# Moving scores, values and a projection's halves in the TensorE order of three turns

## The chip, the cores and the metric

The kernel runs on one core of a Trainium2 chip. The metric is the device time of one execution in microseconds, as the median of three runs. The core has five engines that work from queues of their own, each strictly in the order in which its instructions stand: TensorE (PE in the profile, with its weight loads as PEld), VectorE (DVE), ScalarE (ACT), GpSimd (POOL) and SyncE (SP, which here only issues DMAs). They wait for each other by semaphores.

## The reference, cut to what matters

Two blocks follow each other. The first is a gated linear attention with a state of 48 by 48 per head: 4 batches, 8 heads, 768 steps.

```
for t in range(S):
    state = alpha[:, :, t, :, None] * state + einsum('bhd,bhe->bhde', k[:, :, t], v[:, :, t])
    y[:, :, t] = einsum('bhd,bhde->bhe', q[:, :, t], state)
```

Its output, heads side by side, is x with 384 columns. The second block projects x to 512 values and 512 gates, runs a first-order recurrence over the values, multiplies with the SiLU of the gates and projects back:

```
proj = x @ w_in;  val, gate = proj[..., :512], proj[..., 512:]
h = a * h + val[:, t, :];  ys[:, t, :] = h          # for every t
out = (gate * sigmoid(gate) * ys) @ w_out
```

All arrays are float32 at this level (the weights come as 64-bit floats and are converted on the chip).

## The kernel before

The steps are cut into 12 groups of 256 steps, three to a batch. One pass of the loop at L1051, called a **turn** here (n = 0 is the first), projects group n and at the same time does the attention of group m = n + 1, so that the two can fill each other's waits. `general` (L19 to L332) is a second version for unusual inputs, chosen by a flag at the end; it doesn't run here.

The attention of a group has these parts, named by the helpers:

- **Preparation on VectorE**, `products` (L656): alpha is transposed (`turn`, L594), P is a running product over it (`scan_P`, L625), k is transposed, V is a running sum from the other end (`scan_V`, L642), Zk is k times V, q is transposed, Zq is q times P. For groups 4 and up these are seven steps of a generator; `go(count)` (L978) issues the next ones, so its place in the code is their place in VectorE's queue. They are the steps for group n + 2. For groups 1 to 3 the transposes are done on TensorE (`turned`, L684), in one of two forms: as transposes (L689, L690), or as matmuls with the identity (L694).
- **Scores**, `first(m)` (L1031): `scores` (L733) are 32 matmuls of 48 by 64 by 112 into two fixed banks and two rotating ones. `masks` (L748) follows: VectorE masks one half (A, L759), ScalarE copies the other (AK, L760) and GpSimd masks it (L762), ScalarE copies the parts for the states (K, L764).
- **Values and states**, `second(m)` (L1036): `values` (L766) needs both masked halves; `states` (L795) makes the new parts of the state, which ScalarE copies (dS, L818) and GpSimd adds up (`add_up`, L820). In the first two groups VectorE adds them instead (`add_banks`, L832).
- **Carried**, `third(m)` (L1042): the products of q with the added-up states (`carried`, L782) and the rest of the values, then `join` (L900), which brings the result to xT over ScalarE and DMAs on SyncE and GpSimd.

The projection has four parts, `project(n, cc)` (L915). Each is three matmuls of 128 by 128 by 256 for the values into one bank and three for the gates into another; VectorE runs the recurrence over the values (hh, L932), ScalarE the SiLU of the gates (sg, L940), and the returned function multiplies the two (f, L942), on VectorE in the first two turns and the last, on GpSimd else. `output(n)` (L945) is 16 matmul passes of 384 columns and two copies.

A float32 matmul stands in the trace as two passes, each with a weight load; a transpose stands as one.

**What sets the order.** The whole fast version is under a manual schedule: the order of the Python calls is the order on every engine. The rotating banks are four (`ps_mm`), taken in pairs: two calls later the same pair comes again, and its new user waits until VectorE and ScalarE have read the old content. So projection 3 of a turn waits for hh and sg of projection 1 of that turn, and projection 2 for those of projection 0.

In turns 2 to 10 the order on TensorE is: second(m), project 0, 1, 2, 3, third(m), first(m + 1), output(n). In turn 2 first(3) stands at the turn's beginning (L1125), and projection 0 of that turn goes between scores and values. VectorE's steps of `go` come four ahead of projection 0 (one and two in turn 2), then one ahead of each further projection.

Of the kernel before, what the change touches and what calls it, by code (L numbers as in the profile page):

```python
# [346 lines left out]
def fast(  # L347
# [22 lines left out]
    nc = tc.nc  # L370
# [9 lines left out]
    NK = DM // C  # L380
# [300 lines left out]
    def bank_pair(tag=None):  # L681
        return [bank(tag and f"{tag}{i}") for i in range(2)]

    def turned(m, name, js, t):  # L684
        raw = steps_of(name, m)
        tp = t[:, 0:len(js) * C].rearrange("p (j x) -> p j x", j=len(js))
        if (m, name) in ((1, "k"), (1, "q"), (3, "a")):
            for n, j in enumerate(js):
                nc.tensor.transpose(tp[:, n], raw[:, ds(ROW + j * D - 64, C)], ident)  # L689
                nc.tensor.transpose(tp[0:64, n], raw[:, ds(j * D, 64)], ident)  # L690
            return tp.rearrange("p j (c h) -> p h c j", h=4)
        for n, j in enumerate(js):
            for i in range(2):
                nc.tensor.matmul(tp[ds(64 * i, 64), n], raw[:, ds(i * ROW + j * D, 64)], ident,  # L694
                                 start=True, stop=True, skip_group_check=True)
        return tp.rearrange("p j (c h) -> p h c j", h=4)
# [69 lines left out]
    def values(m, across):  # L766

        v_sb = vs[m % NV]
        if across:
            ys[m] = [t.rearrange("p (e t) -> p e t", e=2) for t in bank_pair("y")]  # L770
        for c in range(G):
            for e in range(2):
                for h in range(2):
                    i = 1 - h if across else h
                    for s in range(2):
                        p = 2 * e + (s ^ i)
                        rows = ds(L * h, L)
                        nc.tensor.matmul(ys[m][i][ds(64 * s, 64), e, ds(c * C + h * L, L)],  # L778
                                         v_sb[rows, c, 4 * i + p, :], As[i][rows, c, p, :],
                                         start=across and c == 0 and e == 0, stop=False, skip_group_check=True)  # L780
# [131 lines left out]
    prev_h = [None] * NI  # L912
    fs = {}

    def project(n, cc, late=False):  # L915
# [10 lines left out]
        for vg, kk in order:  # L926
            nc.tensor.matmul((pv, pg)[vg], w_ins[cc][:, kk, vg, :], xT[:, kk, :],  # L927
                             start=(kk == 0), stop=(kk == NK - 1))
        hh = p2.tile([C, GC], FP32, tag=f"h{cc}", name="hh")

        def scan():
            nc.vector.tensor_tensor_scan(  # L932
                out=hh, data0=a_dec[:, cc:cc + 1].to_broadcast([C, GC]), data1=pv,
                initial=prev_h[cc][:, GC - 1:GC] if n % NG else 0.0, op0=ALU.mult, op1=ALU.add)
            prev_h[cc] = hh

        if not late:
            scan()
        sg = p2.tile([C, GC], FP32, tag="sg", name="sg")
        nc.scalar.activation(sg, pg, AF.Silu)  # L940
        engine = nc.vector if n < 2 or n == N - 1 else nc.gpsimd
        f = lambda: engine.tensor_mul(fs[n][cc], sg, hh)  # L942
        return (scan, f) if late else f
# [34 lines left out]
    def go(count):  # L978
        for _ in range(count):
            next(steps, None)  # L980
# [15 lines left out]
    for js, part in zip(halves, parts):  # L996
        copy_turned(tk, js, part)
    low(0)
    parts = [turned(1, "q", js, bank()) for js in halves]
    convert(0)  # L1000
    nc.gpsimd.memset(raws["a"][0:1, 0:1], 0.0)
    load_steps("a", 2, [nc.sync])
# [4 lines left out]
    st = states(0)  # L1007
# [34 lines left out]
    def third(m):  # L1042
        if m < N:
# [4 lines left out]
            if m >= NG:  # L1048
                add_up(m, (3,))

    for n in range(N):  # L1051
        m = n + 1
        if n == 0:
# [17 lines left out]
            convert(3)  # L1071
            junk(1)
            low(4)
            f2 = project(n, 2)
            values(m, True)
            st = states(m)
            add_banks(m, st)
            alphas(3)
            third(m)
            for name in "qa":  # L1080
# [42 lines left out]
        else:  # L1123
            if n == 2:
                first(m)  # L1125
                go(1)
                f0 = project(n, 0)
                second(m)
                go(2)
            else:  # L1130
                second(m)
                go(4)
                f0 = project(n, 0)
            f0()
# [93 lines left out]
```

## Time and profile before

| what | us |
| --- | --- |
| median of 3 runs | 279.72 (278.26 to 280.07) |
| the profiled execution | 279.43 |
| its span, first to last instruction | 277.7 |
| TensorE busy | 268.8 |
| VectorE busy | 218.3 |
| GpSimd busy | 122.4 |
| ScalarE busy | 108.6 |

The profiled execution ran 1.7 us longer than its span, and its time is 0.3 us below the median. All times in rows count from the span's start. A row of the chain of waits has start, duration and what ran or was waited for; "issue" is time in which the trace shows nothing to wait for. A row of the timeline has start, duration, engine, line, operation, output and inputs with their shapes, and in brackets the idle time before it. Matmuls are pipelined, so the rows of the chain, which give each group's part of the elapsed time, are better for sums than the durations of single ones. The clock granted to TensorE was 1.0 throughout.

### The profile page before, as it was taken

How to read it: one execution, taken by the hardware profiler on the slowest of the kernel's cores; microseconds unless marked ns; L12 is line 12 of the kernel's file. 1: busy time of each engine (PE TensorE's matmuls, PEld its weight loads, DVE VectorE, ACT ScalarE, POOL GpSimd, SP SyncE). 2: the span in 40 equal slices, each digit the busy share in tenths (PEclk: the TensorE clock that was granted, in tenths of full speed). 3: DMA queues.
4: the chain of work that ended last, by engine and by line, in shares of the span. 5: the costliest groups of instructions: out<-in, count | busy, mean ns of one | idle time of the engine just before them, and what ended most of it. 6: DMA issues, size and time to landing. Idle time of an engine off the chain costs nothing.

```text
span 277.7 us, 9598 instructions
## 1 busy us (share of the span) xinstructions
PE 268.8 (97%) x4056; PEld 217.0 (78%) x4056; DVE 218.3 (79%) x281; ACT 108.6 (39%) x244; POOL 122.4 (44%) x141
## 2 busy tenths in 40 slices
PE   7999999999989999899999999999999999999995
PEld 5988887876678688488688688688688688787874
DVE  7979998898798995995895995996995993079540
ACT  2577763461332532341542433433434425213111
POOL 8141223130068574563473584484384476435000
PEclk9999999999999999999999999999999999999999
DMA  6949993845919777487468587576687501201201
GB/s 196 295 140 309 296 262 78 205 88 139 267 48 238 149 199 182 103 214 163 103 181 199 114 205 164 130 197 155 152 186 159 144 0 27 77 1 33 71 5 59
DMA packets 51599, 41.18 MB, mean 148 GB/s; under 512 B 27360, under 2 KB 49536, under 8 KB 51552
## 3 DMA queue, kind: packets, MB, share of 16 engines
q1 hardware_dynamic: 48752, 37.50, 53.1%
q0 software_dynamic: 1408, 2.03, 2.8%
q10 hardware_dynamic: 1392, 0.99, 1.2%
q8 instruction: 33, 0.54, 0.9%
q14 instruction: 14, 0.11, 0.2%
HBM read 32.54 MB, written 4.72 MB: 134 GB/s over the span
## 4 chain that ended last, share of the span: by engine, by line
PE 92%; DVE 3%; DMA 1%; POOL 1%; issue 1%; ACT 1%; SPq 0%; DVEq 0%; ACTq 0%
PE mm L927 45%; PE mm L956 21%; PE y L791 4%; PE y L778 4%; PE mm L744 3%; PE s L744 3%; PE s L810 3%; PE mm L694 2%; PE mm L1189 2%; DMA raw_a<-in_alpha_dram 1%; POOL AK L762 1%; DVE P L630 1%; DVE V L649 1%; PE mm L689 1%; PE y L862 1%
## 5 line engine op out<-in xcount | busy, mean ns | idle before, releaser
L927 PE MATMUL mm<-xT,w_in 128*128 128x256 f32 x576 | 128.9, 382 | 0.6 <-ACT xT L884 0.6
L927 PEld LDWEIGHTS mm<-xT,w_in 128*128 128x128 f32 x576 | 108.1, 190 | 16.3 <-issue 0.8
L956 PE MATMUL mm<-w_out,f_last 128*128 128x384 f32 x160 | 54.1, 492 | 1.3 <-DVE A L759 1.3
L940 ACT ACTIVATE sg<-mm 128x256 f32<-128x256 f32 x48 | 18.4, 384 | 85.8 <-PE mm L927 80.3
L956 PEld LDWEIGHTS mm<-w_out,f_last 128*128 128x128 f32 x160 | 29.7, 190 | 21.1 <-issue 1.4
L830 POOL TENSOR_TENSOR sum<-sum,dS 128x192 f32<-128x192 f32 x30 | 33.2, 1108 | 27.3 <-PE mm L927 13.5
L942 POOL TENSOR_TENSOR f_last<-sg,hh 128x256 f32<-128x256 f32 x36 | 30.9, 862 | 30.6 <-ACT sg L940 23.1
L932 DVE TENSOR_TENSOR_SCAN hh<-a_dec,hh,mm 128x256 f32<-128x256 f32 x32 | 23.4, 732 | 15.4 <-PE mm L927 15.2
L630 DVE TENSOR_TENSOR_SCAN P<-al,lower 128x1028 f32<-128x1028 f32 x12 | 31.1, 2595 | 0.6
L649 DVE TENSOR_TENSOR_SCAN V<-al,ends 128x1028 f32<-128x1028 f32 x12 | 28.3, 2356 | 0.4
L907 POOL DMA_DIRECT2D xT<-yst x40 | 20.5, 517 | 13.1 <-ACT yst L904 11.8
L950 ACT ACTIVATE o_sb<-mm 128x384 f32<-128x384 f32 x22 | 10.8, 491 | 38.4 <-PE mm L956 38.4
L762 POOL TENSOR_TENSOR AK<-AK,mask 128x512 f32<-128x512 f32 x9 | 13.2, 1464 | 17.2 <-ACT AK L760 17.2
L759 DVE TENSOR_TENSOR A<-s,mask 128x256 f32<-128x256 f32 x9 | 3.8, 425 | 21.5 <-PE s L744 21.5
L557 POOL TENSOR_TENSOR w_in<-w_in,wr 128x768 int32<-128x768 int32 x4 | 7.3, 1826 | 26.0 <-DVE wr L555 17.0
L595 DVE STREAM_TRANSPOSE k<-raw_k 128x1024 f32<-128x1024 f32 x9 | 18.3, 2033 | 0.0
L595 DVE STREAM_TRANSPOSE q<-raw_q 128x1024 f32<-128x1024 f32 x9 | 18.2, 2022 | 0.0
L778 PEld LDWEIGHTS y<-AK,v 64*64 64x64 f32 x352 | 12.1, 134 | 6.4 <-issue 5.0
L595 DVE STREAM_TRANSPOSE al<-raw_a 128x1024 f32<-128x1024 f32 x8 | 16.3, 2041 | 0.1
L778 PE MATMUL y<-AK,v 64*64 64x64 f32 x352 | 14.5, 221 | 1.0 <-POOL AK L762 1.0
L791 PEld LDWEIGHTS y<-Zq,sum 48*64 48x64 f32 x656 | 11.8, 134 | 4.3 <-issue 4.1
L791 PE MATMUL y<-Zq,sum 48*64 48x64 f32 x656 | 14.4, 221 | 0.6 <-issue 0.6
(158 smaller groups left out, 392.2 us busy)
## 6 DMA issues: line engine op xcount, KB each, us to landing
v<-in_v_dram SPq DMA_DIRECT2D x22, 192.0 KB, 3.3
out_dram<-o_sb SPq DMA_DIRECT2D x22, 192.0 KB, 2.1
raw_k<-in_k_dram SPq DMA_DIRECT2D x18, 184.0 KB, 3.4
raw_q<-in_q_dram SPq DMA_DIRECT2D x18, 184.0 KB, 3.8
raw_k<-in_k_dram SPq DMA_DIRECT2D x18, 176.0 KB, 3.8
raw_q<-in_q_dram SPq DMA_DIRECT2D x18, 176.0 KB, 4.1
raw_a<-in_alpha_dram SPq DMA_DIRECT2D x16, 184.0 KB, 5.0
raw_a<-in_alpha_dram SPq DMA_DIRECT2D x16, 176.0 KB, 5.1
```

The costliest lines, as they stand in the source:

```text
L595: nc.vector.transpose(out=by_runs(to).rearrange("p h c j -> p h j c"), in_=raws[name][:, 0:4 * ROW].rearrange("p (h j d) -> p h j d", h=4, ...
L630: nc.vector.tensor_tensor_scan(out=P, data0=al[:, 0:4 * GP], data1=lower.rearrange("p h t -> p (h t)"), initial=0.0, op0=ALU.mult, op1=ALU ...
L649: nc.vector.tensor_tensor_scan(out=V[:, ::-1], data0=al[:, 1:4 * GP + 1][:, ::-1], data1=ends.rearrange("p h t -> p (h t)")[:, ::-1], init ...
L778: nc.tensor.matmul(ys[m][i][ds(64 * s, 64), e, ds(c * C + h * L, L)], v_sb[rows, c, 4 * i + p, :], As[i][rows, c, p, :], start=across and ...
L791: nc.tensor.matmul(ys[m][i][ds(64 * s, 64), e, ds(u * L, L)], Ss[j][rows, p, :], Zqs[m % 2][rows, u, p, D:], start=False, stop=True, skip_ ...
L830: nc.gpsimd.tensor_add(Ss[j][:, :, 0:D], Ss[j - 1][:, :, 0:D], part)
L907: engines[n % len(engines)].dma_start(out=xT[to, a], in_=st[rows, i, e])
L927: nc.tensor.matmul((pv, pg)[vg], w_ins[cc][:, kk, vg, :], xT[:, kk, :], start=(kk == 0), stop=(kk == NK - 1))
L932: nc.vector.tensor_tensor_scan(out=hh, data0=a_dec[:, cc:cc + 1].to_broadcast([C, GC]), data1=pv, initial=prev_h[cc][:, GC - 1:GC] if n % ...
L940: nc.scalar.activation(sg, pg, AF.Silu)
L942: f = lambda: engine.tensor_mul(fs[n][cc], sg, hh)
L956: nc.tensor.matmul(os[c], fs[n][cc][:, ds(c * C, C)], w_outs[cc // 2][:, cc % 2, :], start=(cc == 0), stop=(cc == NI - 1))
```

## The change

Four things are moved; nothing is added to or taken from what is computed.

1. **Start**: the second half of q of group 1 is turned by eight matmuls with the identity instead of eight transposes.
2. **Turn 0**: projection 2 is parted. Its three value matmuls and the recurrence come first, then values and states of group 1 and the additions of the states, then its three gate matmuls and the SiLU.
3. **Turns 2 and 4** (the third and the fifth): values and states of groups 3 and 5 stand behind projection 1 instead of behind projection 0 (turn 2) or ahead of it (turn 4). In turn 4 two of the four `go` steps now stand behind projection 0. The functions f of projections 0 and 1 come ahead of `add_up` on GpSimd in both turns.
4. **Turn 3** (the fourth): the scores of group 5 and their masks stand behind output 3 instead of ahead of it.

```
-        if (m, name) in ((1, "k"), (1, "q"), (3, "a")):
+        if (m, name) in ((1, "k"), (1, "q"), (3, "a")) if by_transpose is None else by_transpose:
...
-    parts = [turned(1, "q", js, bank()) for js in halves]
+    parts = [turned(1, "q", js, bank(), js is halves[0]) for js in halves]
...
+        passes(order[:NK] if between else order)
...
         if not late:
             scan()
+        if between:
+            between()
+            passes(order[NK:])
         sg = p2.tile([C, GC], FP32, tag="sg", name="sg")
...
+    late = (1, 3)
...
-            f2 = project(n, 2)
-            values(m, True)
-            st = states(m)
-            add_banks(m, st)
+            def across_and_states():
+                values(m, True)
+                add_banks(m, states(m))
+
+            f2 = project(n, 2, between=across_and_states)
...
             if n == 2:
                 first(m)
-                go(1)
-                f0 = project(n, 0)
-                second(m)
-                go(2)
-            else:
+            if n - 1 not in late:
                 second(m)
                 go(4)
-                f0 = project(n, 0)
+            else:
+                go(n // 2)
+            f0 = project(n, 0)
             f0()
+            if n - 1 in late:
+                go(2)
             load_raw("k", n + 3, nc.sync)
             load_raw("a", n + 3, nc.sync)
             go(1)
             f1 = project(n, 1)
             f1()
+            if n - 1 in late:
+                second(m)
...
             third(m)
-            first(m + 1)
+            if n not in late:
+                first(m + 1)
             load_v(m + 2, nc.sync)
...
         if 0 < n < N - 1:
             output(n)
+        if n > 1 and n in late:
+            first(m + 1)
```

More of the change, by code (lines that the diff above doesn't have):

```diff
@@ L682, in bank_pair, with turned @@
         return [bank(tag and f"{tag}{i}") for i in range(2)]
-    def turned(m, name, js, t):
+    def turned(m, name, js, t, by_transpose=None):
         raw = steps_of(name, m)
         tp = t[:, 0:len(js) * C].rearrange("p (j x) -> p j x", j=len(js))
-        if (m, name) in ((1, "k"), (1, "q"), (3, "a")):
+        if (m, name) in ((1, "k"), (1, "q"), (3, "a")) if by_transpose is None else by_transpose:
             for n, j in enumerate(js):
@@ L913, in fast, with project @@
     fs = {}
-    def project(n, cc, late=False):
+    def project(n, cc, late=False, between=None):
         if cc == 0:
@@ L925, in project, with passes @@
             order.sort(key=lambda x: x[1])
-        for vg, kk in order:
-            nc.tensor.matmul((pv, pg)[vg], w_ins[cc][:, kk, vg, :], xT[:, kk, :],
-                             start=(kk == 0), stop=(kk == NK - 1))
+        def passes(part):
+            for vg, kk in part:
+                nc.tensor.matmul((pv, pg)[vg], w_ins[cc][:, kk, vg, :], xT[:, kk, :],
+                                 start=(kk == 0), stop=(kk == NK - 1))
+        passes(order[:NK] if between else order)
         hh = p2.tile([C, GC], FP32, tag=f"h{cc}", name="hh")
```

## The prediction

> **What bounds the kernel now.** I read the page first: busy time of the engines, and the chain of work that ended last.
>
> ```profile
> PE 268.8 (97%) x4056; PEld 217.0 (78%) x4056; DVE 218.3 (79%) x281; ACT 108.6 (39%) x244; POOL 122.4 (44%) x141
> ...
> PE 92%; DVE 3%; DMA 1%; POOL 1%; issue 1%; ACT 1%; SPq 0%; DVEq 0%; ACTq 0%
> ```
>
> TensorE is the bound: 92% of the chain is on it. The order is all that is changed, so there is nothing to gain but TensorE's idle time, 277.7 - 268.8 = 8.9 us, and most of that lies at the start and the end. Next I read what TensorE waited for (who waited for whom: total, times, longest):
>
> ```profile
> PE mm L956 <- DVE A L759: 1.3, 1, 1.3
> PE y L778 <- POOL AK L762: 1.0, 1, 1.0
> PE y L791 <- issue: 0.6, 1, 0.6
> ```
>
> Three holes, 2.9 us, and each lies where the change acts. The chain in order of time (start, us, what) shows the places: turn 0, turn 2, turn 3.
>
> ```profile
> 43.50 0.65 issue
> ...
> 74.40 0.84 PE mm L744 x32
> ...
> 75.88 3.04 POOL AK L762
> ...
> 78.97 0.69 PE y L778 x32
> 79.66 0.72 PE s L810 x64
> 80.38 7.97 PE mm L927 x36
> 88.35 0.39 PE y L791 x16
> ...
> 89.20 0.47 PE y L791 x32
> ...
> 110.02 0.77 PE s L744 x32
> ...
> 112.05 0.77 issue
> 112.81 5.40 PE mm L956 x16
> ...
> 130.09 0.39 PE y L791 x16
> ...
> 131.65 0.77 PE s L744 x32
> ...
> 133.19 5.36 PE mm L956 x16
> ```
>
> So the first question is what each move does to its hole; the second, what it does to VectorE, which is busy 79% and has little room in a turn.
>
> **Start (q half).** Eight transposes go, eight matmuls of two passes come.
>
> ```profile
> 16.90 0.11 PE mm L689
> ...
> 32.40 3.64 PE mm L694 x64
> ```
>
> 8 x 0.11 = 0.88 us against 16 x 3.64/64 = 0.91: **+0.03**. ScalarE copies the result in both cases.
>
> **Turn 0 (projection 2 parted).** The order of VectorE and GpSimd stays. Values and states start half a projection earlier (7.97/3 = 2.66 for a whole one, so 1.3 us); the gates fill the time after them, and ScalarE's SiLU moves 1.4 us back (values and states, 0.69 + 0.72), ahead of alpha's copies, which wait for the transposes anyway. By itself that is no time. But the hole at 43.50 lies in the middle of a run of equal matmuls (L791), with nothing to wait for, so I asked what the DMAs carried just before it, and counted the passes from that hole to the one of turn 3 (a stretch: length, then busy time and number per engine; DMA by queue, packets, MB, share, for 41.4 to 42.8 and 109.9 to 111.3):
>
> ```profile
> 43.24:111.21 67.97, 66.24 (x1028) 52.82 (x1023) 58.27 (x66) 25.45 (x59) 29.12 (x28) 1.00 0.67 159
> ```
> ```profile
> q8 instruction: 1, 0.02, 5.5%
> ```
> ```profile
> q8 instruction: 1, 0.02, 5.2%
> ```
>
> One packet of instructions came shortly before each hole, and the holes are 1028 + 1023, some 2050, instructions of TensorE apart. I take both as late program: a run of short matmuls uses up what is there before the next packet comes. [...] The parted projection puts 1.3 us of long matmuls into the stretch before the hole of 0.65 us: **-0.65**; bounds 0 (the packet comes as late as before, as it shares the DMAs with the loads) and -0.65, the whole hole.
>
> **Turn 2 (values behind two projections).** Before, projection 0 ended at 78.97 - 1.0 = 77.9, and the values waited for GpSimd's mask, done at 78.92. Now projection 1 (7.97/3 = 2.66) fills that: it ends at 80.6; values and states (0.69 + 0.72) at 82.0; projection 2 at 84.7; projection 3 would end at 87.3 in place of 88.35. What is late next? VectorE's order is the same, and the bank pair of projection 3 needs projection 1's recurrence; GpSimd has its sums behind f1 now, which waits for that recurrence too.
>
> ```profile
> 84.23 0.73 DVE L932 TENSOR_TENSOR_SCAN hh<-a_dec,hh,mm 128x256 f32<-128x256 f32 x1
> ...
> 87.35 1.21 DVE L605 TENSOR_TENSOR Zq<-q,P 128x1024 f32<-128x1024 f32 x1
> ```
> ```profile
> 83.23 2.21 POOL L830 TENSOR_TENSOR sum<-sum,dS 128x192 f32<-128x192 f32 x2
> ...
> 87.59 1.56 POOL L942 TENSOR_TENSOR f_last<-sg,hh 128x256 f32<-128x256 f32 x1 [0.77 <-DVE hh L932]
> ```
>
> The recurrence is done at 84.96, against 84.7 for projection 3; in the built order it is the gates of projection 3 that use the bank it frees, 1.3 later, so there is no wait. f1 runs 85.1 to 85.8. The sums take some 0.6 each where nothing is beside them: the pair at 83.23 ends 2.21 later, of which 1.1 lie under VectorE's multiplication by V (83.1 to 84.3). Three of them are done at 87.6, unless Zq at 87.35 stops the third: f at 87.59 took 1.56 beside Zq, where another (109.02, below) took 0.73. Then it ends at 88.7. The third sum is needed at 87.3 + 0.39, 0.47 for the rest of the values and half of the 0.47 at 89.20, 88.4. So **-1.05 + 0.3 = -0.75**, between -1.05 and 0. [...]
>
> **Turns 3 and 4 (scores behind output 3).** Output 3 can start when the carried part ends at 110.02: the last f was done before, and the hole of 1.3 us ahead of 112.81 goes. The late program, if it is that, then has 5.4 us of long matmuls ahead of it.
>
> ```profile
> 109.02 0.73 POOL L942 TENSOR_TENSOR f_last<-sg,hh 128x256 f32<-128x256 f32 x1 [1.28 <-ACT sg L940]
> ```
>
> But the masks are ahead of the next preparation in VectorE's queue. Before, VectorE went from the masks to alpha at 112.18, beside output 3. Now the masks wait for the scores, these for output 3, and behind them the whole preparation of group 6 waits too. VectorE's rows of that turn, and turn 2's, where scores already follow an output (that of turn 1, ending at 73.47):
>
> ```profile
> 110.84 0.42 DVE L759 TENSOR_TENSOR A<-s,mask 128x256 f32<-128x256 f32 x1 [2.95 <-PE s L744]
> ...
> 112.18 2.05 DVE L595 STREAM_TRANSPOSE al<-raw_a 128x1024 f32<-128x1024 f32 x1
> ...
> 114.29 2.74 DVE L630 TENSOR_TENSOR_SCAN P<-al,lower 128x1028 f32<-128x1028 f32 x1
> ...
> 121.74 0.73 DVE L932 TENSOR_TENSOR_SCAN hh<-a_dec,hh,mm 128x256 f32<-128x256 f32 x1
> ...
> 123.73 0.75 DVE L932 TENSOR_TENSOR_SCAN hh<-a_dec,hh,mm 128x256 f32<-128x256 f32 x1
> ...
> 126.98 1.20 DVE L605 TENSOR_TENSOR Zq<-q,P 128x1024 f32<-128x1024 f32 x1
> ```
> ```profile
> 73.47 0.93 PE s L744 x32
> ```
> ```profile
> 75.56 2.29 DVE L630 TENSOR_TENSOR_SCAN P<-al,lower 128x1028 f32<-128x1028 f32 x1
> ```
>
> From the end of output 3, called 0: VectorE is free of masks at 75.56 - 73.47 = 2.1. From alpha's start to the end of projection 1's recurrence it needs 124.48 - 112.18 = 12.3, less 0.45 as P, 2.74 here, took 2.29 in turn 2: 11.85, whichever recurrence stands where. So that recurrence ends at 13.95. TensorE meanwhile: scores 1.77 (0.93 + 0.84), projections 0 and 1 5.3, values and states 1.41, projection 2 2.65: done at 11.15. Projection 3 needs the bank that the recurrence frees: **TensorE waits 2.8**, until 13.95. Then projection 3 (2.65), carried (1.56, from 130.09 to 131.65) and scores (1.54, to 133.19): output 4 starts at 19.7 after output 3's end, 5.36 + 19.7 = 25.05 after 110.02. Before it started at 133.19, 23.17 after. **+1.9** for both together, the closed hole counted. Bounds: +1.5 if VectorE is 0.4 quicker; +2.4 if P takes 2.74 again. Zq is done 3.7 after the recurrence (128.18 less 124.48), 17.65, ahead of the scores at 18.15. GpSimd's sums for this group stand behind f1, from 14.8 to 16.6, in time for the carried part at 16.6.
>
> Alpha of group 7 is loaded behind k's, which waits for the late transpose of k:
>
> ```profile
> 121.11 2.71 SPq L410 DMA_DIRECT2D raw_a<-in_alpha_dram  x4
> ```
> ```profile
> raw_a<-in_alpha_dram SPq DMA_DIRECT2D x16, 184.0 KB, 5.0
> ```
>
> It landed by 123.82 + 5.0 = 128.8, needed once the masks of turn 4 are done, 0.4 after 133.19. Now it lands 5.4 later, 134.2, and is needed 0.4 after 110.02 + 25.05, at 135.5: hidden by 1.3.
>
> **The sum**: +0.03 - 0.65 - 0.75 + 1.9 = +0.5. On the profiled 279.43 (span 277.7 and 1.7 around it) that is 279.95; on the median 279.72 it is 280.25. I take 280.1.
>
> **The rivals.**
>
> 1. *VectorE has room enough, and only the holes go*: -0.65 - 1.05 - 1.3 and 0.2 back for scores behind an output (1.77 against 1.54), 2.8, so 276.8 from the mean of profiled time and median. For it: VectorE idles about 3 us in each turn ahead of the masks. Against it: the count above puts 16 us of preparation behind a start that is 5.4 us later.
> 2. *Late program stays or moves*: the holes of 0.65 and 1.3 come back at other places, 280.1 + 1.9 at the most; one of them, 280.7 to 281.4. For it: which run of short matmuls outruns a packet hangs on the number of instructions ahead of it, and eight transposes become sixteen passes. Against it: after the change more of the short runs have projections between them.
> 3. *GpSimd's sums become the wait* (slower than before): in turns 2 and 4 they stand behind f1 and thus behind VectorE's recurrence. If Zq stops one of them in both turns, carried waits 88.7 - 88.4 = 0.3 in turn 2 and up to Zq's length, 1.2, in turn 4, and f2 and f3 come as much later at the output. It decides if the second sum isn't done when Zq starts. 280.1 + 1.2 to 1.5, some 281.5.
> 4. *The program is never late*: a cause that the trace doesn't name makes the hole at 43.50, it stays, and turn 0 gives nothing: 280.1 + 0.65 = 280.75. For it: the row says only "issue". Against it: the packet before it, and the like hole 2050 instructions later. [...]
>
> **How the numbers follow.** My forecast has 0.5, rival 1 0.1, rival 2 0.13, rival 3 0.17, rival 4 0.1. A measurement of this kernel can tell about 1%, 2.8 us, from no change (its three runs differ by 1.8). (276.9 is 1% under the median, 282.5 is 1% over it.) Under 276.9 lies half of rival 1 and little else: 0.07. Over 282.5 lie the ends of rivals 2 and 3 together: 0.1. Within: 0.83. The range leaves out rival 1 and the joint worst cases: 278.3 (the forecast with the sums not in the way and VectorE at its quickest, and a low median) to 282.2 (forecast, +0.5 from P, and rival 3 or 2).
>
> **What would show it.** In the profile after: no hole at L791 near 43.5 and none at output 3; no wait of values for GpSimd's mask in turn 2; a long idle of VectorE, some 8 us, ahead of the masks of turn 3, where there were 2.95; and, as the decisive row, a wait of TensorE's projection for VectorE's recurrence of 2 to 3.3 us in turn 4. If that row is missing, rival 1 is right; a hole marked "issue" elsewhere speaks for rival 2; a wait of L791 for GpSimd's sum for rival 3. I am wrong most easily in VectorE's chain: 0.5 us on it is 0.5 us of time.

## The result, and the profile after

The changed kernel took 286.14 us (median of 6 runs, 285.6 to 287.15) against 279.7 for the kernel before on the same chip: a ratio of 1.025 (95% interval 1.023 to 1.0269), some 2.5% slower. The forecast was 280.1, with a range up to 282.2. The profiled execution took 285.6, its span is 283.9, and before it was 277.7: there are 6.2 us to find.

First the page's busy times and its clock row, in 40 slices of 7.1 us:

```profile
PE 271.4 (96%) x4064; PEld 217.9 (77%) x4064; DVE 217.9 (77%) x281; ACT 108.8 (38%) x244; POOL 119.1 (42%) x141
...
PEclk9999799999999999999999999999999999999999
```

TensorE has the eight matmuls more that were expected (4064 against 4056), but is busy 2.6 us longer, and in the fifth slice its granted clock was not full. Before, it was full throughout. Who waited for whom:

```profile
PE mm L928 <- ACT junk L623: 3.2, 1, 3.2
PE mm L928 <- DVE hh L935: 2.4, 1, 2.4
...
PE mm L810 <- issue: 1.0, 1, 1.0
```

The three holes of before (L791, the values behind GpSimd's mask, output 3) are gone. The wait for the recurrence, 2.4, is the one that the forecast named as decisive (2.8). But two waits are new, both in the first turn, and the chain shows where (start, us, what):

```profile
20.19 1.01 issue
21.20 0.24 PE mm L810 x2
...
26.86 1.14 ACT junk L623 x2
28.00 0.61 issue
28.62 6.16 PE mm L928 x20
34.78 1.90 PE mm L694 x32
...
49.65 0.77 PE s L744 x32
...
78.65 0.93 PE s L744 x32
...
95.61 4.71 PE mm L962 x14
...
114.42 5.36 PE mm L962 x16
...
139.36 0.84 PE mm L962 x2
```

(L928 and L962 are the old L927 and L956, the projection and the output.) The releaser named for the second wait, `junk`, is a scratch result that no projection reads: a sign that the profile found nothing better. It is a wait in the middle of a projection's 24 passes, after the fourth, and the passes behind it are slow: 6.16 us for 20, where 24 took 5.42 before. The clock is in the windows (stretch: length, then busy time and number for PE, PEld, DVE, ACT, POOL; granted clock; DMA share; GB/s):

```profile
25.81:29.22 3.41, 0.60 (x3) 0.55 (x3) 1.09 (x2) 2.17 (x4) 0.00 (x0) 1.00 1.01 331
29.22:32.64 3.42, 3.42 (x9) 2.71 (x9) 1.76 (x3) 0.97 (x2) 0.00 (x0) 0.50 0.95 239
32.64:36.05 3.41, 3.41 (x34) 2.86 (x34) 2.75 (x5) 0.90 (x3) 0.52 (x1) 1.00 0.89 315
```

Behind the wait the granted clock was 0.50 for 3.41 us. The cost is put at half of that, 1.7, an estimate: at 5.42 for 24, the 20 passes would have taken 4.52, 1.64 less than they did. From the rows shown of both profiles, stage by stage:

| stage, from and to | before | after | difference | forecast |
| --- | --- | --- | --- | --- |
| start, to alpha's transposes (L694 x32) | 28.81 | 34.78 | +5.97 | +0.03 |
| turn 0 from there, to the scores at 44.54 / 49.65 | 15.73 | 14.87 | -0.86 | -0.65 |
| turn 2, from the scores at 73.47 / 78.65 to output 2 at 91.21 / 95.61 | 17.74 | 16.96 | -0.78 | -0.75 |
| turns 3 and 4, from 110.02 / 114.42 to output 4 at 133.19 / 139.36 | 23.17 | 24.94 | +1.77 | +1.9 |

(44.54 is 43.50 and the hole of 0.65 and 0.39 of L791; output 2 of before starts at 91.21 by its chain.) The rest adds 0.1. So the three terms of the moves are as forecast to 0.2 us; the whole error is in the first line.

The ratios given below leave out runs over 1.5% above the fastest of their kernel; as these are a part of the finding here, the spread of all runs is given as well.

### The profile page after: what moved, and what is told of

Same layout as the page of the kernel before. It is cut to its first block, busy times and chain, and to the rows that moved or that the text cites. A ratio compares the mean times of both kernels' runs of the same rounds, so it can differ in the third digit from the quotient of the medians.

```text
span 283.9 us, 9611 instructions
## 1 busy us (share of the span) xinstructions
PE 271.4 (96%) x4064; PEld 217.9 (77%) x4064; DVE 217.9 (77%) x281; ACT 108.8 (38%) x244; POOL 119.1 (42%) x141
## 4 chain that ended last, share of the span: by engine, by line
PE 87%; DMA 5%; DVE 3%; issue 2%; ACT 2%; ACTq 0%; SPq 0%; DVEq 0%
PE mm L928 43%; PE mm L962 21%; PE y L791 4%; PE y L778 4%; PE s L744 3%; PE mm L744 3%; PE s L810 3%; DMA raw_q<-in_q_dram 3%; PE mm L694 2%; DMA raw_k<-in_k_dram 2%; PE mm L1202 2%; DVE V L649 1%; DVE al L595 1%; DVE k L595 1%; PE y L862 1%
## 5 line engine op out<-in xcount | busy, mean ns | idle before, releaser
L928 PE MATMUL mm<-xT,w_in 128*128 128x256 f32 x576 | 131.5, 386 | 6.1 <-ACT junk L623 3.2
L928 PEld LDWEIGHTS mm<-xT,w_in 128*128 128x128 f32 x576 | 109.0, 192 | 22.9 <-issue 4.1
L962 PE MATMUL mm<-w_out,f_last 128*128 128x384 f32 x160 | 54.2, 492 | 0.0
L948 POOL TENSOR_TENSOR f_last<-sg,hh 128x256 f32<-128x256 f32 x36 | 33.1, 922 | 40.3 <-DVE hh L935 23.4
L962 PEld LDWEIGHTS mm<-w_out,f_last 128*128 128x128 f32 x160 | 29.7, 190 | 19.8
L830 POOL TENSOR_TENSOR sum<-sum,dS 128x192 f32<-128x192 f32 x30 | 29.4, 980 | 21.4 <-ACT dS L818 11.8
L956 ACT ACTIVATE o_sb<-mm 128x384 f32<-128x384 f32 x22 | 10.8, 491 | 37.4 <-PE mm L962 33.0
L605 DVE TENSOR_TENSOR Zq<-q,P 128x1024 f32<-128x1024 f32 (+1 forms) x14 | 15.0, 1069 | 0.0
L614 DVE TENSOR_TENSOR Zk<-k,V 128x1024 f32<-128x1024 f32 (+1 forms) x14 | 14.8, 1054 | 0.1
L778 PE MATMUL y<-A,v 64*64 64x64 f32 x352 | 14.5, 221 | 0.0
```

The source lines that it names most:

```text
L830: nc.gpsimd.tensor_add(Ss[j][:, :, 0:D], Ss[j - 1][:, :, 0:D], part)
L962: nc.tensor.matmul(os[c], fs[n][cc][:, ds(c * C, C)], w_outs[cc // 2][:, cc % 2, :], start=(cc == 0), stop=(cc == NI - 1))
```

## The experiments

Three questions: is the loss at the start due to the q half; what makes it late; and is the loss in turn 4 due to VectorE's queue?

**The parts alone.** `q_half_alone` is the kernel before with only the line of the q half:

```
-    parts = [turned(1, "q", js, bank()) for js in halves]
+    parts = [turned(1, "q", js, bank(), js is halves[0]) for js in halves]
```

> The kernel before with one part of the change alone: the second half of q of group 1 turned by eight matmuls with the identity. Theory (late program): these are 16 more TensorE instructions ahead of the state matmuls of group 0, so that the run of short matmuls reaches the end of its loaded program before the next packet is there, and the packet after it queues behind the loads that start at 19 us. The whole loss of the start, 6.0 us in the profile, comes with this edit alone: 279.7 + 6.0 = 285.7, with a hole of about 1 us near 20, one of about 3 us near 25 and the clock at 0.5 for some 3 us. Rival (the loss is made by the moves of turns 0 to 4 together, the start's holes are chance): 279.7 + 0.03.

Measured: 280.25 (279.18 to 283.72, 10 runs), ratio 1.0029 (1.0001 to 1.0058). The theory missed: this is no 285.7. But six runs lie at 279.2 to 280.3, three at 281.6 and one at 283.7. The profiled one has the two holes at the same places, only small (chain):

```profile
20.04 0.44 issue
...
24.70 0.45 issue
```

`moves_without_q` is the changed kernel with that line as before.

> The changed kernel with q of group 1 turned as before; the parted projection, the values behind two projections and the scores behind output 3 stay. Theory (late program): no hole at 20 and 25, the rest as in the profile of the changed kernel: 279.7 - 0.86 (turn 0) + 0.07 - 0.78 (turn 2) + 1.77 (turns 3 and 4) = 279.9. Rival (the moves make the loss): 285 to 286.

Measured: 280.21 (279.91 to 283.09, 10 runs), ratio 1.0043 (1.0016 to 1.0071); as expected. Six runs are at 279.9 to 280.2 and four at 281.0 to 283.1; the profiled one, 281.22, is of the latter. No hole at the start. Its clock was halved at another place, behind the wait for the recurrence (idle until 127.34):

```profile
124.03:127.45 3.42, 0.96 (x5) 0.51 (x5) 3.42 (x6) 0.38 (x1) 0.02 (x1) 1.00 0.98 223
127.45:130.86 3.41, 3.41 (x9) 2.69 (x10) 3.41 (x3) 0.00 (x0) 3.25 (x5) 0.50 1.03 232
```

So q half and moves give +0.6 each, together +6.4. That is no sum, so the next question was whether the same program always has the same start.

`pad_16` is the kernel before with four small matmuls between the q halves, whose results are not used:

```
+    keep_warm(4, 8)
```

> The kernel before with four small matmuls (8 columns, of zeros, into a bank that nobody reads then) between the two halves of q of group 1: 16 more TensorE instructions at the same place, q turned by transposes as before. Theory (late program): only their number counts, so the holes near 20 and 25 and the slow clock come as with the change: 279.7 + 6.0 and up to 0.4 for the matmuls themselves, 285.7 to 286.1. Rival (it is the form of the matmuls or what they wait for): 279.7 + 0.4.

Measured: 281.19 (280.78 to 282.76, 5 runs), ratio 1.0085 (1.0049 to 1.0121). A hole of 0.43 in the first projection, as with the q half alone. So 16 instructions of another kind bring a hole there too, but not one of 3 us, and the time is far below the 285.7 expected: a miss as well.

**The changed kernel again.** `after_again` and `after_third` are the changed kernel itself, on two chips.

> The changed kernel itself, on the same chip and in the same runs as the next ones. If the late packets at the start belong to the program, all runs are at 285.5 to 287.2, with waits of 1.0 and 3.2 us of TensorE between 20 and 29 us and the granted clock at 0.5 behind them. If they are a matter of the single run, as the spread of the q half alone suggests (279.2 to 283.7), runs from 280 to 286 turn up.

> The changed kernel once more, for how often its start is late. Theory (a race of a few tenths of a us between the second packet and the loads, per run): runs in two groups, 280 to 282 and 285.5 to 287.5, with none between 283.5 and 285; which group is the larger may differ from chip to chip. Rival (the first chip was the odd one): all runs at 280 to 282.

Measured: `after_again` 280.47 (280.21 to 285.88, 5 runs), `after_third` 282.25 (280.03 to 287.79, 9 runs), ratios 1.005 (1.0031 to 1.007) and 1.0069 (1.004 to 1.0099). With the six first runs that makes 20: ten at 280.0 to 282.6 and ten at 284.6 to 287.8. **The changed kernel has two starts.** The profile of `after_again` (span 278.8) has none of the two holes and its stages of turns 0, 2 and 3 to 4 take 14.87, 16.97 and 24.94, as above; its start is still 0.82 us longer than that of the kernel before, as alpha's transposes begin at 29.63. The profile of `after_third`, a run of 287.79, has both holes. First the row of `after_again`, then two of `after_third`:

```profile
29.63 1.90 PE mm L694 x32
```
```profile
PE mm L928 <- ACT junk L623: 2.9, 1, 2.9
PE mm L810 <- issue: 1.0, 1, 1.0
```

**What makes the program late.** For the second hole the views of the DMAs give a cause (queue, kind: packets, MB, share). In the first profile of the changed kernel, no packet of instructions started between 20.0 and 26.1, and the next one came right then:

```profile
q1 hardware_dynamic: 967, 1.75, 89.3%
```
```profile
q1 hardware_dynamic: 187, 0.31, 92.4%
q8 instruction: 1, 0.02, 5.0%
```

(20.0 to 26.1, then 26.1 to 27.3.) That packet, of 16 KB, starts at 26.20, and TensorE goes on at 28.62. In the kernel before, it starts at 21.60. What the DMAs moved meanwhile is data; the loads that SyncE issues at that time, in the changed kernel and in `after_again`:

```profile
18.95 1.19 SPq L421 DMA_DIRECT2D raw_a<-in_alpha_dram  x2
20.19 1.13 SPq L453 DMA_DIRECT2D wbits<-in_moe_w_in_dram  x2
```
```profile
21.30 1.12 SPq L453 DMA_DIRECT2D wbits<-in_moe_w_in_dram  x2
```

TensorE went on in its new block (21.20 above, 20.84 in `after_again`) at the end of the issue of w_in in the one, and before it in the other.

The first hole needs another cause, which these views do not show. The packet that TensorE waits for at 20.19 started at 18.48, 1.59 us after TensorE had gone into the block ahead of it (counted as in the table below), and the DMAs carried almost nothing meanwhile: their share was 0.06 from 17 to 18 and, with the packet itself, 0.04 from 18 to 20 (the last number but one).

```profile
18.00:20.00 2.00, 2.00 (x117) 1.83 (x113) 1.10 (x2) 1.22 (x2) 1.37 (x3) 1.00 0.04 8
```

In the three profiles of the changed kernel the start goes with this packet: it took 1.59 and 1.61 us where the hole of 1.0 and the late start followed, 0.72 in `after_again`, where neither did. Without that hole TensorE would have gone on at 20.19 in the first profile and at 20.98 in `after_third`, no later than the issue of w_in began there (20.19 and 21.12). Why this packet was late stays open. The next experiments shift the new block and the loads against each other.

`loads_later` is the changed kernel with those loads (alpha's third group, w_in's third unit) behind the first states, some 3 us later; `win_later` moves w_in alone, behind k, q and alpha.

> The changed kernel with the loads of alpha of group 2 and of the last w_in columns issued some 3 us later (behind the conversion of w_in 1 on GpSimd, near 22 instead of 19). Theory (the second packet is late because it queues behind these loads): the first hole of 1.0 stays, the second of 3.2 and the slow clock after it (1.7) go: 286.1 - 4.9 = 281.2, up to 283 if something waits for the later loads. Rival (the packet is late whatever the loads do): 286.1 or more.

> The changed kernel with the load of the third unit of w_in alone issued some 3 us later, behind the steps of k, q and alpha; alpha's load stays where it is. Theory (the second packet stands behind w_in's 2 x 768 KB): it starts within 3.5 us of the crossing, the hole of 3.2 shrinks to under 1 and the clock stays up: 281 to 282. Rival (it stands behind whatever load is there, alpha's and k's too): 285 to 286.5.

Measured: `loads_later` 281.52 (281.4 to 283.42, 4 runs), ratio 1.0101 (1.0052 to 1.015). The time is as expected, but the first hole, which was to stay, is gone too: its packet came after 0.3 us in the profiled run. So this run does not test the loads alone. The two packets after the third now meet the loads, with holes of 0.3 and 0.5. `win_later` 285.88 (282.69 to 288.23, 6 runs), ratio 1.0249 (1.0222 to 1.0276): a miss. Five of six runs are at 285.3 and more. Only the quickest run has a profile, with holes of 0.7 and 0.5 at the start; the packet of the second started 2.3 us after TensorE had gone into the block ahead, with alpha's and k's steps issued by then and no w_in. So w_in is not the only load that goes with a late packet, and what the slower runs waited for is not shown.

`count_restored` and `after_less` take TensorE's blocks back, by alpha's second group: its first half, or both, as transposes, 16 or 32 instructions fewer.

```
-            copy = copy_turned(to, js, turned(m, name, js, bank(tag)), ...
+            copy = copy_turned(to, js, turned(m, name, js, bank(tag), True if (m, name, n) == (1, "a", 0) else None), ...
```

> The changed kernel with the first half of alpha's second group by eight transposes in place of sixteen passes: 16 instructions of TensorE fewer ahead of the start's short passes, so that every block boundary stands at the instruction where it stood before the change; the q half stays as changed. Theory (the count of instructions decides): no hole over 0.4 us at the start, 280.0 (279.7 + 0.3 for the moves), up to 281.7 in runs where the wait for the recurrence in turn 4 halves the clock. Rival (the kind of the q half's instructions, or what they do to the copies, decides): 285.5 to 287.

> The changed kernel with both halves of alpha's second group by transposes: 32 instructions of TensorE fewer at the start than the change has, 16 fewer than before it. Theory (the place of the block boundary against the loads decides, and fewer instructions ahead of it are better): no late start in any run: 279.9 to 280.6, and 281.2 to 282.6 in the runs where the wait for the recurrence in turn 4 halves the clock. Rival (every shift of the boundaries off the old place brings it): runs at 285.5 to 288 as well.

Measured: `count_restored` 280.49 (280.35 to 282.47, 5 runs), ratio 1.0083 (1.005 to 1.0116), `after_less` 281.94 (280.67 to 282.69, 6 runs), ratio 1.0087 (1.0055 to 1.0118). None of the 11 runs is at 284 or more; the five higher ones (281.6 to 282.7) have a mean clock of 0.993 or 0.994, one halving, and in the profile of `after_less`, one of these, it stands behind the wait for the recurrence. So it is not the kind of the q half's instructions that matters but where the blocks end; the evidence is 0 late starts in 11 runs against 10 in 20, and on the chip of `count_restored` the changed kernel itself had one in five. `count_restored` is 1.5 us over the kernel before on its chip, where 0.3 was expected. `after_less` is no better than `count_restored`: a hole of 0.5 has come at another place of the start, and its lower runs, 280.7 to 281.5, are 0.1 to 0.9 over what was expected.

`extra_load` is the kernel before with 1.5 MB more in line, from memory to memory, between alpha and w_in.

```
+    for vg in range(2):
+        nc.sync.dma_start(out=out.bitcast(U32)[3 - vg, 0:4 * C]..., in_=moe_w_in.bitcast(U32)...)
     load_w(units[2], nc.sync)
```

> The kernel before with two more transfers of 768 KB, from memory to memory, between the loads of alpha and of w_in's third unit; TensorE's program is the same, instruction by instruction. Theory (a packet of instructions stands behind the data that is in line): the third packet, that comes 1.3 to 2.1 after its crossing in the kernel before, comes 4 to 7 after it, TensorE has a wait of 2 to 5 us without a data cause between 24 and 30 us, and the clock falls to 0.5 behind it. Besides, the data of group 2 comes 4 to 6 later, for which k's transposes wait some 1 to 4. In all 283 to 290. Rival (packets don't stand behind data): waits of TensorE for data only, the packet at its old distance.

Measured: 285.54 (285.04 to 286.66, 4 runs), ratio 1.024 (1.0205 to 1.0274). The time is as expected, the reason is not: the packet came 2.9 after TensorE had gone into the block ahead of it, not 4 to 7, and no hole without a data cause lies at the start. TensorE waits for w_in's data instead, over a conversion in ScalarE's queue:

```profile
PE mm L744 <- ACT sg L940: 3.8, 1, 3.8
```
```profile
22.25 12.24 DMA wbits<-in_moe_w_in_dram
```

More data in line is not enough, then. What is different shows when the profiles stand side by side: the moment at which TensorE goes on in the new block (found by counting its instructions in blocks of 256 from the hole at 20.19: of the records of its weight loads, matmuls and semaphore instructions, 705 start ahead of that hole and 961 ahead of the one before 28.62, and in the kernel before 1729 and 3777 ahead of those at 43.50 and 112.05), the time in which SyncE issues w_in, and how long after that moment the packet starts.

| kernel | TensorE goes on | w_in issued | packet starts, after that |
| --- | --- | --- | --- |
| loads_later | 20.25 | 23.11 to 24.23 | 1.15 |
| steps_less | 20.07 | 20.15 to 21.27 | 1.5 |
| scores_behind | 20.09 | 20.15 to 21.27 | 2.05 |
| parted_two | 20.99 | 21.28 to 22.40 | 1.2 |
| before | 20.34 | 20.56 to 21.68 | 1.25 |
| after_again | 20.84 | 21.30 to 22.42 | 1.45 |
| count_restored | 21.15 | 20.87 to 21.99 | 1.35 |
| steps_ahead | 20.33 | 20.14 to 21.26 | 1.7 |
| moves_without_q | 20.27 | 20.13 to 21.25 | 2.6 |
| q_half_alone | 20.48 | 20.14 to 21.26 | 2.2 |
| pad_16 | 21.05 | 20.60 to 21.72 | 2.5 |
| after_less | 21.18 | 20.43 to 21.55 | 3.0 |
| idle_act | 20.64 | 19.84 to 20.97 | 4.1 |
| after_third | 21.99 | 21.12 to 22.24 | 4.5 |
| after, first profile | 21.20 | 20.19 to 21.32 | 5.0 |

The order is not strict: `scores_behind` waits 2.05 with no w_in issued, `count_restored` 1.35 with a quarter of it. But on the whole, the more of w_in was issued, the later the packet, as if it stood behind what was issued until then and not behind what comes after. In `extra_load`, only a third of the extra data was. So the last test exchanges the two loads in the kernel before, with the same program for TensorE and the same bytes (a small memset on w_in's buffer holds its load until 18.8), and in the changed kernel:

```
+    nc.gpsimd.memset(wbits[units[2]][0:1, 0, 0, 0, 0:1], 0)
+    load_w(units[2], nc.sync)
     load_steps("a", 2, [nc.sync])
-    load_w(units[2], nc.sync)
```

> The kernel before with the loads of w_in's third unit and of alpha's third group exchanged: w_in is issued from 18.95 to 20.1, alpha behind it. TensorE's program and all bytes are as before. Theory (a packet is asked for when TensorE goes into a new block, and stands behind the w_in data that was issued until then; over the profiles so far it came 1.2 to 2.1 after that moment where w_in was issued later, 2.2 to 3.0 where it was half issued, 4.1 to 5.0 where it was nearly all issued): the third packet comes 4 to 5 after the crossing at 20.3 in place of 1.3, and a wait of 0.5 to 1.3 us without a data cause lies in the first projection near 25.8: 0.5 to 1.3 over the kernel before. Rival (the order of the loads is nothing to it): packet and time as before.

> The changed kernel with the same exchange. Theory: TensorE goes into the block at 20 to 21.2, behind the whole issue of w_in, in every run, so that the slow start comes in nearly all of them: 284.5 to 288. Rival: the two groups as without the exchange, 10 of 20 runs at 280 to 282.6.

Measured: `win_first` 280.29 (279.68 to 281.01, 10 runs), ratio 1.0034 (1.0024 to 1.0045), +0.8 us, as expected. In its profile, of the quickest run, w_in is issued from 18.81 to 19.71, TensorE goes on at 20.62, the packet starts 4.4 after that, and the hole is there (chain):

```profile
23.62 2.83 PE mm L927 x12
26.45 0.99 issue
27.44 2.86 PE mm L927 x12
```

`after_win_first` 283.61 (282.97 to 284.25, 4 runs), ratio 1.0151 (1.0127 to 1.0175): all runs alike, but 0.3 to 1.5 us under the range of the theory. Its packet came 3.45 after 20.35, with w_in four fifths issued, for a hole of 1.3; the clock was halved behind the wait for the recurrence, not there. The direction is right; the size was set too high.

**Does the idle time alone halve the clock?** `idle_act` is the kernel before with three idle copies on ScalarE ahead of xT; no program is late at that place.

```
+        for _ in range(3):
+            idle = p1.tile([C, 4 * GP], BF16, tag="junk", name="junk")
+            nc.scalar.activation(idle, als[0][:, 0:4 * GP], AF.Copy)
```

> The kernel before with three idle copies of ScalarE (some 3.3 us) ahead of the first part of xT, so that TensorE stands still there for 3 to 4 us while its program is all there; what the copies write is read by nobody. Theory (a granted clock of 0.5 for 3.4 us follows an idle of that length by itself, and costs 1.7): 279.7 + 3.3 + 1.7 = 284.7, clock 0.994, and in the stretch behind the idle a granted clock of 0.5. Rival (the clock fell for the late program or for the loads): 283.0, clock 1.0.

Measured: 284.4 (282.9 to 285.43, 4 runs), ratio 1.0171 (1.0141 to 1.0201). All four runs have a mean clock of 0.994 or less. The wait, and the windows:

```profile
PE mm L930 <- ACT xT L889: 2.6, 1, 2.6
```
```profile
25.23:28.64 3.41, 1.29 (x6) 1.16 (x7) 1.58 (x2) 3.31 (x7) 0.00 (x0) 1.00 1.02 361
28.64:32.06 3.42, 3.42 (x10) 2.71 (x9) 2.91 (x3) 3.03 (x6) 0.00 (x0) 0.50 0.87 225
```

A wait for data, of 2.6, is enough. The theory holds; the wait was 0.7 shorter than set, and the profiled run has a second halving behind a hole ahead of output 3.

**Turns 0 to 4.** `parted_two` is the parted projection and turn 2's values behind two projections alone; `scores_behind` is the scores behind output 3 alone; `steps_ahead` has all three, without the q half, and with VectorE's next two steps issued ahead of output 3, after the changed kernel:

```
             else:
-                go(n // 2)
+                go(1 if n == 2 else 0)
             f0 = project(n, 0)
...
+        if n > 1 and n in late:
+            go(2)
...
         if n > 1 and n in late:
             first(m + 1)
```

> The parted projection of turn 0 and the values behind two projections of turn 2 alone; the start, and the scores ahead of output 3, as before. By the terms read from the two profiles: -0.86 and -0.78, 1.6 us under the kernel before on the same chip (278.1 beside 279.7); the hole ahead of output 3 (1.3) may go as well if its packet finds more time: 276.8. Rival (the gains come only with the later turns moved): within 0.3 of the kernel before.

> The scores of turn 3 behind output 3 alone, with the order of turn 4 that this needs; start and turns 0 and 2 as before. Theory (VectorE's preparation queued behind the masks): 1.8 us over the kernel before (281.5 beside 279.7), a wait of a projection for the recurrence of 2.4 us in turn 4, and 1.7 more in runs where that wait halves the clock. Rival (the wait comes from the other moves): within 0.5 of the kernel before.

> The parted projection, the values behind two projections and the scores behind output 3, without the q half, and with the next group's steps issued ahead of output 3, so that VectorE prepares beside it instead of standing behind the masks. Theory (turn 4 lost its time in VectorE's queue): turn 0 -0.86, turn 2 -0.78, the hole ahead of output 3 gone and 0.2 given back, -1.1: 277.0, no wait of a projection for the recurrence in turn 4 over 0.5 us. Rival (the scores behind the output cost by themselves): 279.7 to 280.2.

Measured: `scores_behind` 281.79 (280.95 to 282.59, 4 runs), ratio 1.0105 (1.0077 to 1.0133), with the wait for the recurrence at 2.5 us: as expected. `parted_two` 279.24 (277.68 to 281.15, 10 runs), ratio 1.0001 (0.9973 to 1.0028): five runs at 277.7 to 278.5 are 0.6 to 1.4 under the kernel before (279.11), 1.0 on average where the terms have 1.6, four at 280.0 to 280.8 have a mean clock of 0.994 (and one is at 281.15). The profiled one is of the latter: the hole ahead of output 3 has grown, and the clock falls behind it.

```profile
PE mm L962 <- issue: 1.8, 1, 1.8
```
```profile
113.06:116.48 3.42, 3.42 (x6) 1.69 (x6) 3.37 (x4) 0.00 (x0) 0.88 (x1) 0.50 0.68 134
```

`steps_ahead` 276.87 (276.48 to 277.22, 4 runs) against 279.0: ratio 0.9926 (0.9905 to 0.9948), **faster than both kernels**, if by less than 1% than the one before. The time is 0.1 from what was expected, the gain is not: 2.1 us on a chip where the kernel before took 279.0, and 2.7 had been expected from 279.7. The chain has nothing but TensorE's work between outputs 3 and 4, the four projections among it:

```profile
108.40 5.36 PE mm L962 x16
...
115.45 5.38 PE mm L928 x24
...
122.16 5.38 PE mm L928 x24
...
130.63 3.42 PE mm L962 x10
```

From output 3 to output 4 that is 22.23, where the changed kernel takes 24.94 and the kernel before 23.17. VectorE shows why. In the changed kernel, then in `steps_ahead`:

```profile
120.76 0.42 DVE L759 TENSOR_TENSOR A<-s,mask 128x256 f32<-128x256 f32 x1 [7.92 <-PE s L744]
121.52 0.42 DVE L759 TENSOR_TENSOR A<-mm,mask 128x256 f32<-128x256 f32 x1 [0.34 <-PE mm L744]
122.10 2.05 DVE L595 STREAM_TRANSPOSE al<-raw_a 128x1024 f32<-128x1024 f32 x1
```
```profile
106.73 2.04 DVE L595 STREAM_TRANSPOSE al<-raw_a 128x1024 f32<-128x1024 f32 x1
...
108.81 2.30 DVE L630 TENSOR_TENSOR_SCAN P<-al,lower 128x1028 f32<-128x1028 f32 x1
114.74 0.42 DVE L759 TENSOR_TENSOR A<-s,mask 128x256 f32<-128x256 f32 x1 [3.63 <-PE s L744]
```

It stood idle for 7.92 us ahead of the masks (the forecast said some 8) with the preparation queued behind them; with alpha and P ahead of the masks it stands 3.63, and 4.3 us of work are off the path.

`steps_less` is that version with 16 instructions fewer at the start, as in `count_restored`.

> The version with VectorE's steps ahead of output 3, and the first half of alpha's second group by transposes: 16 instructions fewer at the start than before the change. Theory: the hole of 0.23 us that was left at 20.1 goes, 276.7 against 276.9, no run over 278. Rival: within 0.1 of that version, as the start then waits for alpha's steps.

Measured: 277.48 (276.82 to 277.81, 6 runs), ratio 0.9933 (0.9905 to 0.996). No gain over `steps_ahead` can be told; a hole of 0.3 is left in turn 0.

## Why the prediction was right or wrong

- **Start, +0.03: the step that failed.** The time of the matmuls was right, TensorE's instructions were not free. The q half puts 16 more of them ahead of the short passes of turn 0, so a block of program ends earlier, inside these passes. In the first profile the packet for the next block is late and TensorE stands there for 1.01 us; so it goes into the new block only at 21.20, when most of w_in is issued (20.19 to 21.32), the next packet starts 5.0 after that, which costs 3.20 more, and behind that wait the clock is 0.50 for 3.41 us, 1.7 by estimate. Together 5.9 of the +5.97. The forecast had named late program as the cause of the old holes, and rival 2 had the very count ("eight transposes become sixteen passes"), but priced it by the old holes, 1.9 at the most, and held against it that "more of the short runs have projections between them". A hole of one place does not bound one of another place: what it costs hangs on what is in line there and, for the first hole, on a packet whose delay stays open.
- **The forecast for the other start.** In half of the 20 runs the start is on time or little late, and the kernel takes 280.0 to 282.6: eight of these ten lie within the range. That is in part luck. They are 0.9 to 3.5 us over the kernel before on their own chips (279.0 and 279.1), where the forecast had 0.4; in the profile of `after_again` the terms of the moves hold and the start is 0.8 longer. The measured median was of the other start. The q half alone, too, costs little in most runs.
- **Turn 0, -0.65: measured -0.86.** The hole at L791 went, as forecast: it is in no profile with the parted projection, and in five of seven without it (0.3 to 0.65 us). The value is beyond the bound given: L791's passes on both sides of the hole took 0.57 + 0.39, now 0.70 in one piece, and the first transposes 0.15 less, while the parted projection takes 2 x 1.49 for 2.79.
- **Turn 2, -0.75: measured -0.78.** The wait for GpSimd's mask went. The sums took 0.63 each and were done as Zq began (92.6 and 92.5), so the reason for the 0.3 given back was wrong: it was at the scores of group 4, whose first half took 1.00 in place of 0.77, 0.07 late.
- **Turns 3 and 4, +1.9: measured +1.77**, in the changed kernel and alone. The masks hold up the preparation, the recurrence is late, TensorE waits 2.4 to 2.5 for it; 2.8 was forecast. Not foreseen: in some runs the clock is halved behind this wait, for 1 to 2 us more (the profiled runs of `moves_without_q` and `after_less`, 281.22 and 282.51 at a mean clock of 0.994, beside runs at 1.0 of 279.9 to 280.2 and of 280.7 to 280.9).
- **Rivals.** Rival 1 (VectorE has room, 276.8) is wrong for this order. `steps_ahead`, where VectorE gets its room, comes near it: 2.1 us under the kernel before, where the rival has 2.8. Rival 3 (GpSimd's sums) didn't come. Rival 4 (the program is never late) falls with `win_first`: the order of two loads makes a hole in TensorE's unchanged program.
- **Still open:** why the packet ahead of the first hole comes 0.7 us after TensorE had gone into the block ahead in one run and 1.6 in another with the DMAs almost idle (a share of 0.04 to 0.06), and why all six first runs fell on the late side. The reason given for the second hole rests on the table's order and on the exchange of two loads; the packets' place in the line itself can't be seen, and that a packet is asked for when TensorE goes into the block ahead of it is inferred from these times. For a run without a profile, its time is all that is known.

## What to carry to other kernels

A change that adds or removes TensorE instructions moves every later block boundary of its program (the boundaries counted above stand 256 records or a multiple of that apart, in the kernel before and in the changed one at the same counts); ahead of a long stretch of short matmuls beside heavy loads, look at which loads are issued when the boundary is passed, and time the kernel in several calls, on more than one chip, before its median is believed. A step that is put behind a long matmul stretch holds up all that is queued behind it on its engine: move the independent work of that queue ahead of it, as in `steps_ahead`, and the move that cost 1.8 us gains 0.9. Price a hole of 2 us and more at itself and at up to 1.7 more, an estimate from the halvings of 3.41 us that followed 2.1 to 2.8 us of idle time here; behind the wait of 2.4 to 2.5 one came in three profiles and none in six.

## What the runs showed of the hardware

- TensorE's program comes over the DMAs in packets of 16 KB: 33 of them, 0.54 MB (queue q8), stand in each of the profiles of the kernel before and of the changed kernel, for 8209 and 8221 records of TensorE. They can be late: holes of 0.4 to 3.2 us without a data cause in the first projection, where the packet started 2.2 us (`q_half_alone`, a hole of 0.45) to 5.0 us (the changed kernel, 3.2) after TensorE had gone into the block ahead, and of 1.0 us just before, where it started 1.59 and 1.61 us after that with the DMAs almost idle (a share of 0.04 to 0.06). Most block boundaries show no hole: of 32 in each of the two kernels, those at L791 (0.65) and ahead of output 3 (1.3) do in the one, and those of the start (1.0 and 3.2) in the other.
- The halvings of the granted clock that the rows here show, to 0.5, took 3.41 us each. In the changed kernel's first profile the clock fell at 29.22, was back at 32.63 and fell again at 285.22, behind the last instruction, 75 times 3.413 us after the first fall. That it changes only at such steps is a reading of these times, and the stretches given here are steps counted that way. TensorE's idle time in the step ahead of a halving was 2.8 us in the changed kernel (25.81 to 29.22), 2.46 in `moves_without_q` (124.03 to 127.45), 2.12 in `idle_act` (25.23 to 28.64) and, amid the short passes ahead of output 3, 1.8 in `parted_two` (109.65 to 113.06); the second halving of `idle_act` stands behind a hole of 1.5 there. Behind idle times of 1.94 in one step (`loads_later`, 125.45 to 128.87) and of 1.79 (below) there was none. The wait for the recurrence, of 2.4 to 2.5, had a halving behind it in three profiles (`moves_without_q`, `after_less`, `after_win_first`) and none in six (the changed kernel's first, `after_again`, `loads_later`, `count_restored`, `win_later`, `scores_behind`). Where the wait lies in the steps would explain that, an estimate from these rows: in `moves_without_q` 2.46 of it lie in one step, in the changed kernel it is parted:

```profile
128.21:131.62 3.41, 2.76 (x12) 2.10 (x12) 3.36 (x6) 1.10 (x3) 0.00 (x0) 1.00 0.42 112
131.62:135.03 3.41, 1.62 (x8) 1.44 (x9) 3.41 (x3) 0.00 (x0) 1.45 (x3) 1.00 1.06 227
```

This is the wait for the recurrence in the changed kernel's first profile: 0.65 us of it lie in the one step and 1.79 in the next, and the clock stays at 1.0 behind it.
